# Attention and a gated MLP on one core: the first exponentials lie in another tile's memory, and the work is ordered anew

## The chip, the cores and the metric

The kernel runs on one core of a Trainium2 chip. Its engines work side by side, each through its own list of instructions in a fixed order: TensorE (PE; PEld is its weight load) multiplies matrices, VectorE (DVE), ScalarE (ACT) and GpSimd (POOL) work on tiles, and SyncE (SP) starts the DMAs. An instruction that must wait holds up all that stand behind it on its engine. The metric is the time of one execution on the device in microseconds (us), and less is better.

## The reference

The inputs are eight batches of eight heads, with 576 positions of 64 numbers. Queries and keys are first rotated by position ("rope"), then comes attention, and its output is the input of a gated MLP whose weights are the same for all batches:

```python
scores = matmul(rotate(q), rotate(k).T) / 8          # 576 x 576 per head
attn = exp(scores - max(scores)); attn /= sum(attn) + 1e-9
x = heads side by side of matmul(attn, v)            # 576 x 512 per batch
h = maximum(x @ w_in, 0)                             # 512 -> 1024, halves u and v
v_n = (v - mean(v)) / sqrt(var(v) + 1e-6)            # over the 512 features
v_s = w_spatial @ v_n + b_spatial                    # over the 576 positions
out = (u * v_s) @ w_out                              # 512 -> 512
```

## The kernel before

Two heads are worked on together: a *pair*. There are 32 pairs, numbered i = 0 to 31, four to a batch, and after the fourth pair of a batch comes the MLP of that batch, whose products stand between the score tiles of later pairs.

*Pairs 0 to 3* go the plain way. Their scores are fp32 matmuls (L817). VectorE takes the maximum of a score tile (L839), ScalarE the exponential (L842). The exponentials must lie turned for the product with v; TensorE turns blocks of them with matmuls against an identity matrix (function `turned` inside `values_plain`), ScalarE or VectorE copies the result out of PSUM into a slot called `eh`, and TensorE multiplies it with v (L726).

*Pairs from 4 on* go another way. A query or key is split into a high part, rounded by ScalarE (L420, `round_hi`), and a low part, the rest, by POOL (L423, `rest_lo`); the parts lie stacked in three tiles named `stk`, where the keys' parts (`lk`) are copied by DMAs. Scores are L797. VectorE turns the exponentials in blocks of 32 x 32 within their tile `et` (L844), and the product with v is L757: 288 small matmuls in two pieces, whose left operand is `vr`, a copy of v for this pair that four DMAs fill, one for each group of 32 partitions, 320 KB each.

POOL also does the rope (L545, then the sum L549 of its two parts), normalises the attention output (L880), and takes the low parts of all MLP operands: weights `wi`, `wo`, spatial weights `wsp` with their tail `wt`, and the normalised values `vn` (function `norm`). The MLP's spatial product is L955, of `vn` with `wsp`.

*Loads.* SP issues every DMA in one order (L417; the first ones at L599). `st` is the load of a pair's queries (st6_0 of pair 6) or keys (st6_1).

*What sets the order.* The program first lists 4344 operations, each with what it reads and writes, and then carries them out in the order of a table of numbers, `ORDER`; each engine gets its instructions in that order, and a letter behind a number says which engine does an operation that two could do. The buffers are handed out in the same walk: a `Buf` names a pool, `SLOTS` says how many slots the pool has, and the table `HOME` says which slot a new buffer takes. A buffer that takes a slot waits until the last reader of the slot's previous buffer is done.

*The place of the change.* `turns` is one buffer of pool "vrep", the pool of `vr` for pairs from 4 on, which has one slot. In it lie the `eh` slots and, behind them, the identity. `vn` is a tile of its own. The first instructions of the program fill it with constants: POOL fills a piece of `wsp` with zeros, on which TensorE runs matmuls (`wake`, L1032) before its first scores.

Of the kernel before, what the change touches and what calls it, by code (L numbers as in the profile page):

```python
# [8 lines left out]
F32 = mybir.dt.float32  # L9
# [6 lines left out]
P = 128  # L16
# [17 lines left out]
    "stk": 3, "small": 3, "nmx": 3, "rt": 1, "sc": 2, "pm": 4, "eh": 6,  # L34
# [66 lines left out]
4 65 5 2 7 6 12 0 3 1 8 9 10 11 13 15 138 14 16 139 142 70 71 72 74 73 76 79 77 36 75 80 140 81 402 18 78 84 82 85 86 87 83 88 144 91 89 90 100 143  # L101
101a 45 145v 218 59 312 17 96 92 93 130 141g 220 219 308 147 19 20 112 97a 113a 150 21 22 313 94 314 310 309 95a 98 99a 109 103 315 151 148 104a 102
23 149 24 131 105 27 107 110a 37 132 152 106a 108a 126 111 155 123 38 153 127a 121 393 156 214 215 216 217 39 154 40 133 157 41 42 124a 118 122a 28
116 25 114 119a 160 158 117a 29 120 125 128 30 161 159 31 32 162 115 129 60 33 165 170 221 174 171a 167 166 163 164 172 175v 134 135 34 168 420 146
173a 176 177v 169 223 224 206 179 181 311 226 180a 185 182v 183 178 207 208 188 136 137 227 225 228 62 421 427 186a 184v 187 189a 202 428 46 47 229
230 231 232 48 411 43 44 190 191 203v 49 50 194 433 195v 431 316 192 299 51 434 26 193a 233 234 199 435 200a 197 198v 235 236 237 196 201 238 204 54
55 246 209 205 290 241 242 239 240 63 210 247v 243 244 245 282 255 252 253a 257 256v 250 248 251a 436 249a 258v 259 317 283 284 432 291 292 222 211
422 254 61 35 318 264 319 320 321 260v 212 261 262a 293 294 265a 322 285 263 295 323 429 430 747 296 270 213 437 273 324 325 268 266 274v 326 493 269a
271v 327 297 440 267 300 275 301 438 328 272 276a 329 330 331 278 302 277 279v 52 340 303 304 819 305 344 439 753 754 341a 332 345a 333 298 748 755
335 825 337 338 306 280 334 342 343v 441 336 445 446 339 756 346 444 286 442 449 53 281 287 347v 450 353 376 377 447 355 354a 378 356a 451 412 348 413  # L110
457 358 826 359a 351 453 362 458 352a 64 459 363a 452 349 350a 288 461 372 414 307 443 454 455 763 415 759 357 373a 416 364 365a 417 462 448 465 466
369 379 289 367 384 757 380 370a 368a 758 764 456 460 385 366 463 464 423 467 360 468 371 361 426 374 375 820 386 469 470 471 381 382 383 477 760 394
# [210 lines left out]
def tile_attention_gated_mlp(  # L323
# [21 lines left out]
    def T(shape, dt, name):  # L345
        return sb.tile(shape, dt, tag=name, name=name, bufs=1)
# [72 lines left out]
    def round_hi(hi, src):  # L419
        nc.scalar.activation(hi, src, AF.Copy)  # L420
# [702 lines left out]
```

## Time and profile before

| | us |
|---|---|
| three runs | 812.27, 815.41, 815.51 (median 815.41) |
| profiled execution | 813.5 |
| its span, of which the page and the trace tell | 811.7 |
| PE busy | 797.3 (98%) |
| PEld busy | 720.4 (89%) |
| POOL busy | 609.4 (75%) |
| DVE busy | 583.6 (72%) |
| ACT busy | 537.9 (66%) |

The trace is one execution. A time is counted from the start of the span. An engine's idle time matters only where the engine that is nearly always busy, here PE, ends up waiting for it. SPq and POOLq are the issue of instructions by SP and POOL. "<-" behind an instruction names what its engine last waited for, with the line that wrote it.

### The profile page before, as it was taken

What the parts mean: (1) busy time and instruction counts of PE and PEld (TensorE: products, weight loads), DVE (VectorE), ACT (ScalarE), POOL (GpSimd) and SP (SyncE); (2) the same over time, 40 slices, a digit from 0 to 9 for tenths busy, and PEclk for the clock granted to TensorE, in tenths of its full rate; (3) what the DMA queues carried; (4) which work ended last, traced back from release to release, by engine and by line L of the source; (5) the groups of instructions that cost most, each with busy time, mean ns of one, the idle gap of its engine ahead of it and who ended that gap; (6) DMA issues with size and microseconds to landing.
All of it is one profiled execution on the core that took longest, in us unless ns stands there. A gap on an engine that the chain in (4) does not pass through costs nothing.

```text
span 811.7 us, 30045 instructions
## 1 busy us (share of the span) xinstructions
PE 797.3 (98%) x12568; PEld 720.4 (89%) x12568; DVE 583.6 (72%) x1230; ACT 537.9 (66%) x1353; POOL 609.4 (75%) x507
## 2 busy tenths in 40 slices
PE   7999899999999999999999999999999999999998
PEld 3666599998999989999899999999899998999898
DVE  6989897877876588676866778776787767774410
ACT  4988788665875678565775668656686657664442
POOL 7899799976869778798688877887879786644231
PEclk9999999999999999999999999999999999999999
DMA  9456665667765666757746776666566675452101
GB/s 347 181 192 202 154 162 140 173 178 197 169 162 132 170 178 157 196 147 193 201 119 163 177 205 169 161 167 158 166 178 146 168 205 166 109 138 69 44 2 59
DMA packets 53817, 129.86 MB, mean 160 GB/s; under 512 B 7857, under 2 KB 9905, under 8 KB 53682
## 3 DMA queue, kind: packets, MB, share of 16 engines
q1 hardware_dynamic: 53138, 127.35, 57.8%
q8 instruction: 99, 1.62, 0.9%
q10 hardware_dynamic: 544, 0.59, 0.3%
q14 instruction: 36, 0.29, 0.1%
HBM read 93.55 MB, written 9.58 MB: 127 GB/s over the span
## 4 chain that ended last, share of the span: by engine, by line
PE 87%; POOL 4%; DMA 3%; DVE 3%; ACT 1%; issue 1%; SPq 0%; POOLq 0%; DVEq 0%
PE psum L797 16%; PE psum L757 15%; PE psum L955 13%; PE psum L970 13%; PE psum L914 12%; PE psum L937 11%; PE psum L726 2%; PE psum L817 2%; PE psum L680 2%; DMA st<-in_qk_dram 2%; DMA vr<-in_v_dram 1%; DVE nmx L839 1%; POOL st L545 1%; POOL st L549 1%; ACT et L842 1%
## 5 line engine op out<-in xcount | busy, mean ns | idle before, releaser
L842 ACT ACTIVATE et<-psum,nmx 128x576 f32<-128x576 f32 x288 | 212.5, 739 | 98.8 <-DVE nmx L839 96.6
L839 DVE TENSOR_REDUCE nmx<-psum 128x1 f32<-128x576 f32 x288 | 212.6, 744 | 87.6 <-PE psum L797 71.8
L844 DVE STREAM_TRANSPOSE et<-et 128x576 f32<-128x576 f32 x252 | 188.1, 762 | 33.3 <-ACT et L842 31.9
L545 POOL TENSOR_TENSOR st<-st,tabs 128x1152 f32<-128x1152 f32 x56 | 149.6, 2673 | 25.8 <-DMA st<-in_qk_dram 25.1
L757 PE MATMUL psum<-et,vr 32*64 32x144 f32 x8064 | 142.1, 285 | 1.8 <-DMA vr<-in_v_dram 1.8
L757 PEld LDWEIGHTS psum<-et,vr 32*64 32x64 f32 x8064 | 126.5, 130 | 13.6 <-issue 8.5
L955 PE MATMUL psum<-wsp,vn 128*128 128x288 f32 x768 | 127.5, 297 | 0.6 <-POOL wsp L423 0.3
L937 PE MATMUL psum<-x,wi 128*128 128x288 f32 x768 | 125.4, 297 | 0.0
L914 PE MATMUL psum<-wi,x 128*128 128x512 f32 x448 | 119.5, 395 | 0.0
L970 PE MATMUL psum<-g,wo 128*128 128x288 f32 x768 | 117.5, 296 | 0.0
L937 PEld LDWEIGHTS psum<-x,wi 128*128 128x128 f32 x768 | 110.7, 188 | 5.3 <-issue 2.0
L955 PEld LDWEIGHTS psum<-wsp,vn 128*128 128x128 f32 x768 | 110.1, 188 | 2.7 <-issue 1.4
L970 PEld LDWEIGHTS psum<-g,wo 128*128 128x128 f32 x768 | 107.2, 188 | 2.6 <-issue 1.8
L797 PE MATMUL psum<-stk 128*128 128x288 f32 x448 | 99.2, 303 | 1.7 <-ACT et L842 1.2
L797 PE MATMUL psum<-stk,stk 128*128 128x288 f32 x448 | 95.6, 295 | 0.0
L914 PEld LDWEIGHTS psum<-wi,x 128*128 128x128 f32 x448 | 78.7, 188 | 12.2 <-issue 1.2
L423 POOL TENSOR_TENSOR stk<-st,stk 64x512 fp32r<-64x512 f32 x56 | 71.9, 1283 | 20.2 <-ACT stk L420 8.8
L797 PEld LDWEIGHTS psum<-stk 128*128 128x128 f32 x448 | 72.7, 188 | 12.0 <-ACT et L842 4.2
L549 POOL TENSOR_TENSOR st<-st 128x576 f32<-128x576 f32 x56 | 79.9, 1427 | 2.8
L423 POOL TENSOR_TENSOR g<-u,g 128x288 fp32r<-128x288 f32 x64 | 51.0, 809 | 32.5 <-ACT g L420 31.0
L797 PEld LDWEIGHTS psum<-stk,stk 128*128 128x128 f32 x448 | 71.7, 188 | 0.0
L423 POOL TENSOR_TENSOR x<-x,x 128x576 fp32r<-128x576 f32 x64 | 54.5, 874 | 22.4 <-ACT x L420 22.1
(130 smaller groups left out, 1065.2 us busy)
## 6 DMA issues: line engine op xcount, KB each, us to landing
vr<-in_v_dram SPq DMA_DIRECT2D x116, 320.0 KB
st<-in_qk_dram SPq DMA_DIRECT2D x62, 576.0 KB
stk<-lk SPq DMA_DIRECT2D x168, 144.0 KB
out_dram<-ob SPq DMA_DIRECT2D x31, 288.0 KB
ws<-in_w_spT_dram SPq DMA_DIRECT2D x2, 576.0 KB
tabs<-in_tab_dram ACTq DMA_DIRECT2D x2, 288.0 KB
st<-in_qk_dram SPq DMA_DIRECT2D x2, 288.0 KB
wi12raw<-in_w_in_dram SPq DMA_DIRECT2D x1, 512.0 KB
```

The source lines that it names most:

```text
L423: eng.tensor_tensor(out=lo, in0=src, in1=hi.bitcast(F32), op=ALU.subtract)
L545: f = lambda e: e.tensor_tensor(out=st[j][:, cols], in0=st[j][:, cols], in1=tabs[:, cols], op=ALU.mult)
L549: f = lambda e: e.tensor_tensor(out=st[j][:, :S], in0=st[j][:, :S], in1=st[j][:, S:2 * S], op=ALU.add)
L757: nc.tensor.matmul(bank(g)[64 * h:64 * h + 64, EACH // 9 * (1 - h):EACH // 9 * (1 - h) + EACH], lhsT=vr[rows, b % 4, b // 4, h, :], rhs=e[ ...
L797: nc.tensor.matmul(pt[:, c * 512:c * 512 + HALF], lhsT=lhsT, rhs=rhs[:, c * HALF:(c + 1) * HALF], start=(n == 0), stop=(n == len(parts) - 1))
L839: op(DVE, 680, key + K_MAX, lambda: nc.vector.tensor_reduce(out=nmx.tile, in_=tops(), op=ALU.max, axis=AX.XY, negate=True), r=[pt], w=[nmx ...
L842: op(ACT, 750, key + K_EXP, lambda: nc.scalar.activation(weights(), tops(turn), AF.Exp, bias=nmx.tile, scale=1.0, accum_out=sm[:, to:to + ...
L844: op(DVE, 705, key + K_TURN, lambda: nc.vector.transpose(out=blocks(et, at), in_=blocks(et, at)), w=[(et, at)])
L914: nc.tensor.matmul(pm.tile, lhsT=lhsT, rhs=win[1, d][:, j, :], start=(d == 0 and n == 0), stop=(d == 3 and n == len(todo) - 1))
L937: nc.tensor.matmul(pm[:, :HALF], lhsT=win[0, d][:, i, f * P:(f + 1) * P], rhs=x[d][:, at:at + HALF], start=(d == 0 and n == 0), stop=(d == ...
L955: nc.tensor.matmul(pm[:, :HALF], lhsT=lhsT, rhs=rhs, start=(t == 0 and n == 0), stop=(t == 4 and n == 1))
L970: nc.tensor.matmul(pm[:, :HALF], lhsT=wout[d,][:, i, m * P:(m + 1) * P], rhs=gs[d][:, at:at + HALF], start=(d == 0 and n == 0), stop=(d == ...
```

## The change

The buffer `turns` moves from pool "vrep" to a new pool "vn" of one slot, which it shares with `vn`; `vn` becomes a `Buf` that the first rounding of the first MLP opens, and every later user of it names it among what it reads. There are eight `eh` slots in place of six. The tables `ORDER` and `HOME` are written anew, all of them; a line of each is shown.

```diff
-    "stk": 3, "small": 3, "nmx": 3, "rt": 1, "sc": 2, "pm": 4, "eh": 6,
+    "stk": 3, "small": 3, "nmx": 3, "rt": 1, "sc": 2, "pm": 4, "eh": 8, "vn": 1,
...
-4 65 5 2 7 6 12 0 3 1 8 9 10 11 13 15 138 14 16 139 142 70 71 72 74 73 76 79 77 36 75 80 140 81 402 18 78 84 82 85 86 87 83 88 144 91 89 90 100 143
+0 65 5 3 7 1 12 4 6 10 8 9 11 13 15 14 16 2 70 71 72 73 74 75 138 140 139 76 79 80 77 78 81 86 84 85 384 91 82 83 87 88 100 89 90 142 143 144 101a 17
...
-    "00115400600472600176574110650011762253147160402567345176254564570654702645061"
+    "156400117230546070401657031657002145710316522407531642725644756041754036547610"
...
-    vn = T([P, 4, 2, HF], F32R, "vn")
+    vn = Buf("vn", [P, 4, 2, HF], F32R, "vn")
...
-                    need = [("vn", t, 0), ("vn", t, 1), ("wsp", t)] if t < 4 else [("vn", 4, 0), ("vn", 4, 1), ("vn", 4, 2), "wt", "ones"]
+                    need = [vn, ("vn", t, 0), ("vn", t, 1), ("wsp", t)] if t < 4 else [("vn", 4, 0), ("vn", 4, 1), ("vn", 4, 2), "wt", "ones"]
...
-            op(ACT, 520, key, lambda: round_hi(vn[:, t, 0, :], vv.tile), r=[vv], w=[("vn", t, 0)])
-            pair_op(HF, key, lambda e: rest_lo(e, vn[:, t, 1, :], vv.tile, vn[:, t, 0, :]), r=[vv, ("vn", t, 0)], w=[("vn", t, 1)])
+            op(ACT, 520, key, lambda: round_hi(vn[:, t, 0, :], vv.tile), r=[vv, *([vn] if b or t else [])], w=[("vn", t, 0), *([] if b or t else [vn])], new=[] if b or t else [vn])
+            pair_op(HF, key, lambda e: rest_lo(e, vn[:, t, 1, :], vv.tile, vn[:, t, 0, :]), r=[vv, vn, ("vn", t, 0)], w=[("vn", t, 1)])
...
-    turns = Buf("vrep", [P, 6 * CW + P], F32, "turns")
-    ident = lambda: turns[:, 6 * CW:]
+    turns = Buf("vn", [P, 8 * CW + P], F32, "turns")
+    ident = lambda: turns[:, 8 * CW:]
```

Where the instructions stand now is shown at two places. A number behind a name tells buffers of one name apart, and differs between the two programs.

**The four fetches of pair 4's vr, on SP.** In the order before they stand late and two at a time, between copies of pair 5's key parts (stk out of lk5); st6_1 is the load of pair 6's keys:

```order
L417 DMA rb3_931<-rt3d_826 64x576 x2
L417 DMA vr4_948<-in_v_dram 32x4x640 x2
L417 DMA st6_1_967<-in_qk_dram 128x1152
L417 DMA stk0_396<-lk5_893 64x576
L417 DMA stk2_398<-lk5_893 64x576
L417 DMA stk1_397<-lk5_893 64x576
L417 DMA vr4_948<-in_v_dram 32x4x640 x2
L417 DMA stk1_397<-lk5_893 64x576
L417 DMA stk0_396<-lk5_893 64x576
L417 DMA stk2_398<-lk5_893 64x576
L417 DMA st7_0_1280<-in_qk_dram 128x1152
```

In the new order two of them stand here, among early loads of weights (ws2, wi00raw) and of the values of pairs 2 and 3:

```order
L417 DMA ws2_280<-in_w_spT_dram 128x2x576
L417 DMA vr2_318<-in_v_dram 128x640
L417 DMA vr4_352<-in_v_dram 32x4x640
L417 DMA wi00raw_354<-in_w_in_dram 128x1024
L417 DMA rt0d_266<-rt0_267 2x4x128
L417 DMA rt0d_266<-rt0_267 2x1x64
L417 DMA vr3_374<-in_v_dram 128x640
L417 DMA vr4_352<-in_v_dram 32x4x640
```

and the fourth here, ahead of st6_1 again (the third stands between the two places, by itself):

```order
L417 DMA stk0_426<-lk5_925 64x576
L417 DMA wst_1013<-in_w_spT_dram 64x576 x2
L417 DMA wst_1013<-in_b_sp_dram 1x576
L417 DMA st7_0_1024<-in_qk_dram 128x1152
L417 DMA stk2_428<-lk5_925 64x576
L417 DMA stk1_427<-lk5_925 64x576
L417 DMA vr4_352<-in_v_dram 32x4x640
L417 DMA st6_1_1155<-in_qk_dram 128x1152
```

Three fetches have moved from behind pair 4's loads to far ahead of them, and the load of pair 7's queries, st7_0, now stands ahead of the last fetch and of pair 6's keys.

**POOL, the ropes after pair 5's query parts.** In the order before the rope of pair 6's keys (L545, st6_1) stands behind the low part of pair 5's queries for the first of its two stacks (stk0):

```order
L423 TENSOR_TENSOR stk0_396<-st5_0_672,stk0_396 64x512
L545 TENSOR_TENSOR st6_1_967<-st6_1_967,tabs_64 128x1152
L423 TENSOR_TENSOR wo0_1039<-sgwo0_991,wo0_1039 128x512
L423 TENSOR_TENSOR wi03_1042<-sgwi03_886,wi03_1042 128x512
L423 TENSOR_TENSOR stk1_397<-st5_0_672,stk1_397 64x512
```

In the new one the rope of pair 7's queries (st7_0) stands in that place:

```order
L423 TENSOR_TENSOR stk1_427<-st5_0_656,stk1_427 64x512
L423 TENSOR_TENSOR stk0_426<-st5_0_656,stk0_426 64x512
L423 TENSOR_TENSOR wo0_1022<-sgwo0_1005,wo0_1022 128x512
L545 TENSOR_TENSOR st7_0_1024<-st7_0_1024,tabs_64 128x1152
L423 TENSOR_TENSOR ql_74<-st6_0_760,qt_73 64x4x16 x2
L423 TENSOR_TENSOR wo1_1047<-sgwo1_1026,wo1_1047 128x512
```

The two ropes have changed places; that of pair 6's keys now follows four pieces behind it. At the start of the program the fill of the piece of wsp, which stood behind those of wt2, vt2, bias, sums, qt and ql, is now the first on POOL.

**POOL, ahead of the low part of pair 6's queries.** That part is the last row here (stk0<-st6_0). Before:

```order
L423 TENSOR_TENSOR wt2_70<-wst_865,wt1_69 64x576
L423 TENSOR_TENSOR vn_71<-vv0_0_1062,vn_71 128x512
L545 TENSOR_TENSOR st7_0_1280<-st7_0_1280,tabs_64 128x1152
L423 TENSOR_TENSOR wi02_1287<-sgwi02_1187,wi02_1287 128x512
L423 TENSOR_TENSOR lk6_1309<-st6_1_967,lk6_1309 128x576
L423 TENSOR_TENSOR ql_75<-st6_0_743,qt_74 64x4x16 x2
L549 TENSOR_TENSOR st7_0_1280<-st7_0_1280 128x576
L880 TENSOR_TENSOR x32_4_1271<-x32_4_1271,rb4_1334 128x576
L423 TENSOR_TENSOR stk0_396<-st6_0_743,stk0_396 64x512
```

Now:

```order
L423 TENSOR_TENSOR wsp_68<-ws0_820,wsp_68 128x576
L423 TENSOR_TENSOR vn_1176<-vv0_0_1063,vn_1176 128x512
L423 TENSOR_TENSOR wi02_1293<-sgwi02_1187,wi02_1293 128x512
L423 TENSOR_TENSOR lk6_1313<-st6_1_1155,lk6_1313 128x576
L423 TENSOR_TENSOR vn_1176<-vv0_1_1075,vn_1176 128x512
L549 TENSOR_TENSOR st7_0_1024<-st7_0_1024 128x576
L423 TENSOR_TENSOR wt2_70<-wst_1013,wt2_70 1x576
L423 TENSOR_TENSOR vn_1176<-vv0_2_1200,vn_1176 128x512
L880 TENSOR_TENSOR x32_4_1288<-x32_4_1288,rb4_1359 128x576
L423 TENSOR_TENSOR stk0_426<-st6_0_760,stk0_426 64x512
```

A piece of the spatial weights (wsp), two more pieces of the normalised values (vn) and the tail's one row (wt2, 1x576) have come ahead of it; the rope of pair 7's queries has left this stretch.

## Rows read from the trace of the kernel before

**Rows 1.** Stretches: us; PE, PEld, DVE, ACT, POOL busy; PEclk; DMA share; GB/s
```profile
0.00:20.00 20.00, 14.04 (x61) 7.23 (x62) 13.26 (x20) 9.83 (x21) 14.01 (x24) 1.00 0.91 346
20.00:40.00 20.00, 19.77 (x155) 12.01 (x152) 18.29 (x32) 18.23 (x48) 17.92 (x15) 1.00 0.49 180
...
80.00:100.00 20.00, 17.01 (x106) 11.76 (x104) 17.79 (x27) 14.65 (x36) 15.50 (x15) 1.00 0.65 164
100.00:120.00 20.00, 19.12 (x372) 17.25 (x373) 18.13 (x50) 16.67 (x42) 18.77 (x16) 1.00 0.61 151
120.00:140.00 20.00, 19.70 (x392) 18.38 (x391) 16.25 (x37) 16.70 (x45) 19.08 (x14) 1.00 0.49 135
140.00:160.00 20.00, 19.77 (x397) 18.80 (x396) 16.91 (x31) 12.52 (x30) 19.27 (x17) 1.00 0.66 169
160.00:780.00 620.00, 619.67 (x10572) 581.40 (x10571) 443.75 (x960) 406.87 (x1032) 461.78 (x378) 1.00 0.60 158
```

**Rows 2.** Waits of PE, 80 to 160 us: sum us, count, longest
```profile
PE psum L757 <- DMA vr<-in_v_dram: 1.8, 1, 1.8
PE psum L797 <- ACT et L842: 1.7, 2, 1.2
PE psum L955 <- POOL wsp L423: 0.3, 1, 0.3
```

**Rows 3.** Chain of waits around 93 us: start, duration, step
```profile
92.18 1.42 SPq L417
93.65 7.18 DMA vr<-in_v_dram
```

**Rows 4.** Timeline of SP: start, duration, instruction (x: how many in one row)
```profile
87.85 0.82 SPq L417 DMA_DIRECT2D vr<-in_v_dram  x2
88.78 0.96 SPq L417 DMA_DIRECT2D st<-in_qk_dram  x1
```

**Rows 5.** Timeline of PE; in brackets the idle time before, and its releaser
```profile
4.04 5.35 PE L1032 MATMUL psum<-wsp 128*128 128x512 f32 x8 [4.04 <-POOL wsp L388]
9.31 2.52 PE L817 MATMUL psum<-st,st 64*128 64x288 f32 x16
...
84.81 2.95 PE L726 MATMUL psum<-turns,vr 128*64 128x192 f32 x26
...
98.65 0.45 PE L757 MATMUL psum<-et,vr 32*64 32x144 f32 x2
100.88 2.90 PE L757 MATMUL psum<-et,vr 32*64 32x144 f32 x142 [1.77 <-DMA vr<-in_v_dram]
...
106.52 2.51 PE L757 MATMUL psum<-et,vr 32*64 32x144 f32 x144
...
123.77 0.43 PE L797 MATMUL psum<-stk 128*128 128x288 f32 x2
```

**Rows 6.** Chain of waits around 228 us
```profile
227.66 2.83 DMA vr<-in_v_dram
```

**Rows 7.** Timeline of VectorE
```profile
10.68 2.74 DVE L839 TENSOR_REDUCE nmx<-psum 128x1 f32<-128x576 f32 x4
...
97.59 0.76 DVE L844 STREAM_TRANSPOSE et<-et 128x576 f32<-128x576 f32 x1
```

**Rows 8.** Timeline of POOL
```profile
0.74 0.57 POOL L388 MEMSET wt<- 33x576 f32 x1 [0.29 <-POOLq L1111]
...
3.39 0.59 POOL L388 MEMSET wsp<- 128x576 f32 x1
...
96.65 2.67 POOL L545 TENSOR_TENSOR st<-st,tabs 128x1152 f32<-128x1152 f32 x1 [2.76 <-DMA st<-in_qk_dram]
...
107.20 1.28 POOL L423 TENSOR_TENSOR vn<-vv,vn 128x512 fp32r<-128x512 f32 x1
...
117.39 1.29 POOL L423 TENSOR_TENSOR stk<-st,stk 64x512 fp32r<-64x512 f32 x1
...
120.77 1.46 POOL L423 TENSOR_TENSOR wsp<-ws,wsp 128x576 fp32r<-128x576 f32 x1
```

More of the change, by code (lines that the diff above doesn't have):

```diff
@@ L100 @@
 ORDER = """
-4 65 5 2 7 6 12 0 3 1 8 9 10 11 13 15 138 14 16 139 142 70 71 72 74 73 76 79 77 36 75 80 140 81 402 18 78 84 82 85 86 87 83 88 144 91 89 90 100 143
-101a 45 145v 218 59 312 17 96 92 93 130 141g 220 219 308 147 19 20 112 97a 113a 150 21 22 313 94 314 310 309 95a 98 99a 109 103 315 151 148 104a 102
-23 149 24 131 105 27 107 110a 37 132 152 106a 108a 126 111 155 123 38 153 127a 121 393 156 214 215 216 217 39 154 40 133 157 41 42 124a 118 122a 28
-116 25 114 119a 160 158 117a 29 120 125 128 30 161 159 31 32 162 115 129 60 33 165 170 221 174 171a 167 166 163 164 172 175v 134 135 34 168 420 146
@@ L105 @@
[L105 to L112, printed above, removed]
[126 rows of a table removed]
+0 65 5 3 7 1 12 4 6 10 8 9 11 13 15 14 16 2 70 71 72 73 74 75 138 140 139 76 79 80 77 78 81 86 84 85 384 91 82 83 87 88 100 89 90 142 143 144 101a 17
@@ new lines @@
+145v 141g 96 97a 92 93 18 147 308 310 309 312 313 314 19 27 20 150 130 214 216 112 148 94 311 113a 95a 131 98 36 109 502 99a 110a 149 103 104a 21 22
+102 218 220 105 151 107 108a 106a 23 24 132 215 25 37 152 59 38 126 127a 155 156 153 39 154 40 62 121 41 122a 111 123 124a 42 28 157 315 222 160 60
+118 116 119a 117a 158 29 114 30 219 31 32 33 161 159 120 125 423 290 128 115 129 162 133 170 171a 316 165 166 163 164 424 174 299 146 167 175v 43 172
+134 45 176 168 169 173v 221 217 223 179 26 421 135 420 177v 136 137 185 224 180a 186v 226 225 183 206 184a 207 208 227 181 182v 34 188 178 46 47 189v
@@ new lines @@
+228 231 232 187 229 230 48 202 203a 190 427 428 435 436 44 194 195a 433 434 49 192 193a 233 191 50 51 197 198a 234 235 199 200v 236 431 196 201 432
+237 238 204 239 209 210 205 411 241 246 240 242 243 422 35 250 247v 63 244 245 248 282 249a 252 251v 257 255 253v 256a 317 258v 52 291 292 259 260a
+211 318 319 320 293 261 321 294 295 296 426 262a 254 264 322 323 747 748 402 265a 263 429 430 437 440 61 273 325 53 212 213 268 324 270 326 283 284
+285 269v 300 297 274v 266 438 327 271a 267 328 330 301 439 302 303 275 755 272 276a 278 277 329 304 279a 340 331 341a 344 345a 305 332 335 819 337 333
@@ L239 @@
+338 443 336 280 334 342 343v 445 346 339 376 446 441 286 449 347v 450 355 447 377 378 353 356a 54 451 348 354a 457 753 412 281 452 413 458 825 826 358
+359a 351 352a 442 393 448 298 459 453 454 379 754 414 415 349 416 362 363a 287 756 350a 461 364 455 456 417 757 758 372 365a 357 369 462 288 289 444
+465 466 373a 306 763 764 367 368a 366 370a 380 307 385 467 463 460 360 468 371 374 361 375 381 386 464 469 470 471 477 473 382 383 478 479 418 771 761
[126 rows of a table added]
 """
 HOME = (
-    "01070021200103201210302217010126030117512004364541564705001137041472110041753015520100670216130012427310017604554706201001264013005156201073"
@@ L242 @@
-    "54160267011010671524634550110740604100510301015071401201075063141152400120012271000721315440576050415011243305010143011752457400000416110115"
-    "04270103105401002011070400101100160210701512100061103004710100601002013071050411060070123701013146007210600170000114620005141017060051600402"
-    "10501017420101000000176010001151422073011015000014100011170003101650040310010112006511040100051001706010300141050046111013016214000500410020"
-    "05010001710650561047101000001572001000341107006410100501174003010010014020100000000711050401106030111000070140162007000001605010341100110070"
@@ L246 @@
-    "15016407020013005741421001000011067050611500014110001650040010200030511762001100341100700110041101070102100061010000017541100162031015300016"
-    "01000054110205040001760100102015042012703015404007300000116005114500110007161001540020020007041016005210021105010042060011051301000400011170"
-    "06104000001151102307130001400620070000160007015104010301061030117014020060000700115100004114701015060001470160060200070011000651410001210036"
-    "17110400100021107016000510001017101400010123000011654002105200400000013154761000111001161000007314062000000071150040411650011000060160452000"
@@ L250 @@
-    "11000001765102101407001004100630110400002107110060114003201150016130004110105236073001400076000001201054200170101062110004107101006100405117"
-    "00115400600472600176574110650011762253147160402567345176254564570654702645061"
+    "70001120010032012301202712006100111270161523464556042650107013630115460610405715127000170501662173602100700123060451560477650010107140720105"
+    "30741602031710600715246340115576011674701012007166501620130010570415042010021261106020315044365150407101147231746701017051432500010211176004"
@@ new lines @@
+    "42200370051410011200710004006100105111700113001012411001570004040000100116050074111000115110116402530420005030340000115020411007560100504100"
+    "01230056107041010001701160001105067003101021504000100001127000306115100410001200010165041000105300411070006110031500142401011605004000200500"
+    "04120072110601500115740000011576020003000041170601033100115400703010011400001020000071105000103406007111220001407300060010000715106014001000"
+    "10264701540120031520701004000011005671050011040101010645001026001003071641040111050021171010014001070000000021113600011705106011410002703015"
@@ new lines @@
+    "10000714000740000001265102107014000230010715424000700001163005014010516100701310005410110700400001106015201001410520611300041100210050001107"
+    "06120103051140100116210014030706000031006000710015041140601107011500002012400007000116200511700114510015240600070000010041100651170041011242"
+    "01500101600002150001340007100001165010100101023000652104100010450100011040157061001700111061021401370020200060100151040701410500601520041700"
+    "00000000116715001140061120530611001020510070010610015121001006410031050031040210076011400076000001500014000011006123701014000600070001145001"
```

252 rows, old and new, of the table ORDER are left out of this document.

## The prediction

> **What bounds the kernel now.** I read first the table of stretches [rows 1]. From 160 to 780 us TensorE is busy for 619.67 of 620 us: nothing can be won there, and a new order can only lose. Idle time that is not the start or the end lies between 80 and 160 us: 2.99 us in 80 to 100, 0.88, 0.30 and 0.23 us in the next three stretches, 4.4 us in all. In the same place POOL is nearly full too (18.77, 19.08 and 19.27 of 20 us from 100 to 160), so POOL is what could bind next.
>
> Then the waits of TensorE in that place [rows 2]: 1.8 us, once, for a DMA that fills vr; 1.7 us in two waits for an exponential (ACT L842); 0.3 us for POOL's low half of the spatial weights. The first is the place of this change. Tile vr is the copy of v for pair 4, the first pair that doesn't go by transposes. The chain of waits shows how it comes about [rows 3]: the DMA takes 7.18 us, from 93.65 to 100.83 us, and TensorE's products of pair 4 start right behind it.
>
> Why so late? In SP's timeline the first two of the four fetches of vr start at 87.85 us [rows 4]. The last matmul that reads turned exponentials (L726) runs from 84.81 for 2.95 us, to 87.76 us [rows 5]. The memory of vr is the one that holds the exponentials, so the first fetch can't be earlier. And SP issues in order: st, the load of pair 6's keys, stands behind it and goes at 88.78 us.
>
> **The change part by part.**
>
> *Where the exponentials lie.* They move into vn's memory, and vr's memory is free from the start. In the new order three fetches of vr stand far ahead, among loads of pairs 1 to 5, and only the fourth comes late, behind copies of pair 5's keys that wait for the last scores of pair 4. In before two such copies, of about half a microsecond each, stood ahead of the first late fetch, which SP issued at 92.18 us [rows 3]; now it is one. So the late fetch goes at about 91.6 us. Its landing is bounded by two rows: 2.83 us for a lone fetch of the same size at 227.66 us [rows 6], and 7.18 us [rows 3] plus its slow issue, 1.42 us, as it was in the crowd. That gives 94.9 to 100.2 us. I take a value nearer to the lone one, 96 to 98 us: of four fetches in the crowd (320 KB each) one is left, and pair 6's keys stand behind it now.
>
> What is late next? TensorE had done two matmuls of this product at 98.65 us, and stood [rows 5]. The other operand is the last of nine turned tiles, which VectorE gives at 97.59 + 0.76 = 98.35 us [rows 7]; between the maximum of pair 4's seventh score tile and that turn 13 VectorE instructions stand in both orders. So the product starts at 98.65 instead of 100.88: **-2.23 us**, and not more, even where TensorE comes earlier. If the fetch lands at its upper bound, 100.2 us, it is -0.7. The piece behind the wait took 2.90 us for 142 matmuls, and the next product, of 144, took 2.51 [rows 5]: **-0.4 us**, bounded by 0 and -0.4.
>
> *vn becomes a buffer that waits.* The first rounding into vn now waits for the last reader of the exponentials, at 87.76 us. In the trace of before POOL's first work on vn, which follows that rounding, is at 107.20 us [rows 8], some 18 us after the last reader. Cost 0; it would cost only if the MLP's first norm came 18 us earlier.
>
> *Eight slots for turned exponentials instead of six.* No wait of TensorE for such a slot is among its waits from 80 to 160 us; between 20 and 40 us it is busy for 19.77 of 20 [rows 1]. I take 0, bounds -0.2 and +0.2.
>
> *The order, start.* The fill that TensorE's warming matmuls wait for stood behind the other fills on POOL and is now first: it starts at 0.74 instead of 3.39 us [rows 8]. So these matmuls begin at about 1.4 instead of 4.04 us and end at 6.7 instead of 9.39 [rows 5]. The first scores can't use it: the first maximum runs on VectorE at 10.68 us [rows 7], behind VectorE's own rope of pair 0. So 0. But TensorE now stands idle between warming and first scores, for some 1.1 us. [...] Bounds 0 and +1.
>
> *The order, POOL.* Two changes work against each other. In before POOL stood for 2.76 us ahead of the rope of pair 6's keys, waiting for the load that SP held back [rows 8]. Now the rope of pair 7's queries stands there, with its load issued before the late fetch of vr: -2.76 us for POOL. On the other side four more pieces (a half of the spatial weights, two of vn, and the low part of the bias row) now stand ahead of the low part of pair 6's queries: 1.28 to 1.46 us each [rows 8], 5.4 us in all. It ended at 117.39 + 1.29 = 118.68; now 118.68 - 2.76 + 5.4 = 121.3. TensorE's first scores of pair 6 started at 123.77 [rows 5]; 2.6 us earlier is 121.1. Another 0.3 us I add for ACT copies that moved ahead of what POOL reads: **+0.5 us** of new wait. Bounds: 0, and +5 if POOL's idle time comes back (below). The wait of 0.3 us was for the second half of the spatial weights; that now follows one rope and one query part behind 121.3, so it ends near 127 us, some 6 us ahead of the first product that reads it: **-0.3 us**.
>
> *The rest of the order.* From 20 to 80 us the same matmuls stand in nearly the same order, and TensorE is near full; the two waits for exponentials (1.7 us) lie ahead of the product of pair 4, which waits for VectorE anyway. 0, bounds -0.7 and +1. After 160 us 0, bounds 0 and +1.5, since nothing idles there now.
>
> Sum: -2.23 - 0.4 + 0.5 - 0.3 = **-2.4 us**. The profiled execution took 813.5 us, its span 811.7 and 1.8 around it; it would take 811.1. The other three runs are 812.27, 815.41 and 815.51. The mean of all four is 814.2, and minus 2.4 that is 811.8 us, my time. It is a gain of 0.3%; what a measurement of this kernel can tell from no change is about 0.5%, or 4.1 us.
>
> **The rivals.**
>
> *All the idle time goes.* The eight slots and the new order take away the two waits for exponentials and the rest too, and VectorE's turns come as much earlier. For it: it is all one stretch, and VectorE's chain there begins with scores that wait. Against it: VectorE has 17.79 of 20 us there, and its order before the last turn keeps the same count. Price: 4.4 us of idle time [rows 1] and about 1 us in slow starts: 808.8 us from the mean.
>
> *The transfer stays late.* The change doesn't do what it says, since the fourth fetch still stands behind the copies that wait for pair 4's last scores, and it lands at 100.2 us or later. For it: that place in the order, and 7.18 us in the trace. Against it: three quarters of the bytes are gone from that time. Price: only -0.7, and +0.5 for POOL: 814 us.
>
> *POOL becomes the bound, slower than before.* The place is the low part of pair 6's queries. If POOL stands for its loads and for ACT as it did (2.76 us), the end is 118.68 + 5.4 = 124.1, and with 2 to 3 us of waiting for ACT's copies, of which five stand in new places, 126.5; TensorE wanted it at 121.1 and had it by 123.77. It decides from 123.8 us on. Each of pairs 7 and 8 then follows POOL, which has no idle time to catch up. Price: 2.7 us late, and as much again where the order later on has new waits in a stretch that had none: 817 to 819 us.
>
> **How the numbers follow.** The forecast has 0.52, all idle time gone 0.19, the late transfer 0.13, POOL 0.16. The forecast's own range is 809.5 to 814, by the bounds of the landing, the start and the runs' spread of 3 us. For 8 in 10 I leave out the best of the second case and the worst of the last: 807.2 to 816.8 us. Faster than 0.5% takes 810.1: nearly all of the second case and a tenth of the first, 0.23. Slower takes 818.3 or a POOL case with an unlucky run: 0.11. The rest, 0.66, is within 0.5%.
>
> **What would show it.** In the profile after: fetches of vr ahead of 60 us on SP; no wait of TensorE L757 for the DMA near 98 us; VectorE's last turn of pair 4 right before that product; POOL without the 2.76 us ahead of the first rope after 93 us; TensorE's idle time from 80 to 160 us at about 2 instead of 4.4 us. I'd be wrong if the L757 product still starts behind a DMA, if TensorE L797 waits for POOL's stk near 121 us for more than 1 us, if stretches after 160 us show idle time, or if the first maxima come later than 10.7 us.

## The result, and the profile after

The changed kernel took 825.28 us in the median of six runs (822.81 to 828.41), the kernel before 815.19 us in six runs beside it (812.27 to 819.34). The ratio is 1.0125, with a 95% interval of 1.0102 to 1.0148: slower by 1.25%, where 0.3% faster was forecast. The profiled execution has a span of 821.6 us, against 811.7.

The table of stretches answers to [rows 1]; the columns are the same:

```profile
0.00:20.00 20.00, 15.03 (x58) 7.96 (x60) 12.57 (x20) 9.99 (x21) 13.74 (x24) 0.91 0.90 337
...
80.00:100.00 20.00, 18.26 (x234) 13.67 (x237) 18.92 (x32) 18.30 (x46) 16.84 (x18) 1.00 0.60 163
100.00:120.00 20.00, 19.98 (x281) 17.79 (x265) 19.64 (x48) 17.58 (x43) 19.77 (x14) 1.00 0.58 154
120.00:140.00 20.00, 19.27 (x388) 17.70 (x387) 14.57 (x37) 14.08 (x36) 15.44 (x12) 1.00 0.47 135
140.00:160.00 20.00, 18.64 (x384) 17.30 (x383) 16.91 (x32) 11.61 (x29) 18.11 (x15) 1.00 0.46 116
160.00:780.00 620.00, 612.86 (x10502) 573.11 (x10502) 440.03 (x952) 402.29 (x1018) 458.88 (x376) 1.00 0.59 158
```

Read the last row first: TensorE idles for 7.1 us between 160 and 780 us, where it had idled for 0.33. From 80 to 120 us it idles less, 1.8 against 3.9 us, as the change meant it to, and from 120 to 160 more, 2.1 against 0.5. Together that is 3.9 us against 4.4, where the prediction looked for about 2. The granted clock of the first 20 us is 0.91. The waits of TensorE from 80 to 160 us answer to [rows 2] (sum, count, longest); the one for vr is gone, and the second and third are new:

```profile
PE psum L797 <- ACT et L842: 1.7, 2, 1.2
PE psum L955 <- DVE sgwo L467: 1.3, 1, 1.3
PE psum L797 <- POOL stk L423: 0.6, 1, 0.6
PE psum L797 <- issue: 0.2, 1, 0.2
```

From 380 to 780 us no wait of TensorE stood in this table before. Now there are these; a wait for `issue` is one for nothing that the trace shows:

```profile
PE psum L797 <- ACT et L842: 2.3, 2, 1.3
PE psum L955 <- POOL vt L423: 1.5, 1, 1.5
PE psum L955 <- ACT u L940: 1.2, 1, 1.2
PE psum L970 <- POOL g L423: 0.8, 1, 0.8
PE psum L757 <- issue: 0.3, 1, 0.3
PE psum L937 <- ACT vv L988: 0.2, 1, 0.2
```

To see when the time is lost, take in TensorE's timeline the start of the second piece of each pair's product with v (L757), and subtract the start of the same piece before. Negative is earlier, in us; each column is one execution:

| pair (its time before) | changed kernel | old order, new memory | new order up to pair 14, then old |
|---|---|---|---|
| 4 (106.5) | -3.3 | -2.9 | -3.9 |
| 5 (130.1) | -2.3 | -2.9 | -2.9 |
| 6 (155.6) | -0.4 | -3.2 | -2.8 |
| 8 (203.1) | -0.6 | -3.0 | -2.9 |
| 12 (298.2) | -0.6 | -3.7 | -2.3 |
| 16 (392.0) | -0.6 | -3.8 | -0.9 |
| 18 (441.8) | 2.5 | -3.8 | -1.0 |
| 22 (534.8) | 5.6 | -3.8 | -0.9 |
| 27 (650.4) | 7.0 | -3.8 | -0.3 |
| 31 (744.3) | 8.3 | -3.8 | 0.1 |

The last two columns are experiments, below. The changed kernel gains 2 to 3 us at pairs 4 and 5, gives most of it back by 155 us, holds 0.6 us up to 392, and then loses 8.9 us in steps. The waits listed above make some 6 of these 8.9 us; the rest stands in no row of waits. The end adds 1.6 to that (9.9 in the span).

### The profile page after: what moved, and what is told of

Same layout as the page of the kernel before. It is cut to its first block, busy times and chain, and to the rows that moved or that the text cites. A ratio compares the mean times of both kernels' runs of the same rounds, so it can differ in the third digit from the quotient of the medians.

```text
span 821.6 us, 30064 instructions
## 1 busy us (share of the span) xinstructions
PE 800.9 (97%) x12568; PEld 722.3 (88%) x12568; DVE 582.5 (71%) x1229; ACT 539.8 (66%) x1354; POOL 609.2 (74%) x507
## 4 chain that ended last, share of the span: by engine, by line
PE 81%; POOL 7%; DMA 4%; ACT 3%; issue 2%; DVE 1%; SPq 1%; POOLq 0%; ACTq 0%; DVEq 0%
PE psum L797 15%; PE psum L757 14%; PE psum L955 13%; PE psum L970 12%; PE psum L937 10%; PE psum L914 9%; PE psum L726 3%; PE psum L817 3%; PE psum L680 2%; DMA st<-in_qk_dram 2%; DMA out_dram<-ob 1%; POOL st L545 1%; ACT et L842 1%; POOL vn L423 1%; POOL st L549 1%
## 5 line engine op out<-in xcount | busy, mean ns | idle before, releaser
L545 POOL TENSOR_TENSOR st<-st,tabs 128x1152 f32<-128x1152 f32 x56 | 149.3, 2667 | 28.8 <-DMA st<-in_qk_dram 27.6
L757 PE MATMUL psum<-et,vr 32*64 32x144 f32 x8064 | 142.9, 285 | 0.8 <-issue 0.8
L757 PEld LDWEIGHTS psum<-et,vr 32*64 32x64 f32 x8064 | 126.8, 130 | 13.3 <-issue 9.4
L970 PE MATMUL psum<-g,wo 128*128 128x288 f32 x768 | 119.2, 296 | 0.9 <-POOL g L423 0.8
L423 POOL TENSOR_TENSOR stk<-st,stk 64x512 fp32r<-64x512 f32 x56 | 71.8, 1281 | 27.7 <-ACT stk L420 18.1
```

Source lines behind the costliest of these rows:

```text
L423: eng.tensor_tensor(out=lo, in0=src, in1=hi.bitcast(F32), op=ALU.subtract)
L545: f = lambda e: e.tensor_tensor(out=st[j][:, cols], in0=st[j][:, cols], in1=tabs[:, cols], op=ALU.mult)
L757: nc.tensor.matmul(bank(g)[64 * h:64 * h + 64, EACH // 9 * (1 - h):EACH // 9 * (1 - h) + EACH], lhsT=vr[rows, b % 4, b // 4, h, :], rhs=e[ ...
L970: nc.tensor.matmul(pm[:, :HALF], lhsT=wout[d,][:, i, m * P:(m + 1) * P], rhs=gs[d][:, at:at + HALF], start=(d == 0 and n == 0), stop=(d == ...
```

## The experiments

The two orders number the same 4344 operations, so that either can be used with the new memory, whole or in part. `ORDER` and `HOME` go together in all of them, so what is called the order here includes the slots that the buffers take. The runs stand in several groups, each beside the kernel before, whose median was 814.38 to 815.41 us; a difference between two groups is good to about 1 us.

**The new memory with the old order.** The code of the changed kernel, with the tables of before (one entry for vn added to `HOME`).

```diff
-0 65 5 3 7 1 12 4 6 10 8 9 11 13 15 14 16 2 70 71 72 73 74 75 138 140 139 76 79 80 77 78 81 86 84 85 384 91 82 83 87 88 100 89 90 142 143 144 101a 17
+4 65 5 2 7 6 12 0 3 1 8 9 10 11 13 15 138 14 16 139 142 70 71 72 74 73 76 79 77 36 75 80 140 81 402 18 78 84 82 85 86 87 83 88 144 91 89 90 100 143
...
```

> Only the memory is changed: the identity and the turned exponentials lie in vn's memory, eight slots are declared, and the table of the order is the one of before (vn's new entry is added to the table of slots). Theory A (the new order behind 390 us is what costs): no loss, 812 to 816 us beside 815.2, TensorE's idle time from 160 to 780 us below 1 us, and the 1.8 us wait of L757 for vr's DMA shorter or gone. Rival B (the memory itself costs: vn as a buffer that waits, or other addresses): 822 us or more, like the changed kernel. Rival C (the start, with its slow clock): like A here, 812 to 816.

Measured: 811.53 us (809.65 to 812.93), ratio to before 0.9959 (0.9943 to 0.9975). It is faster than both kernels, and the fastest tried. In TensorE's timeline the first piece of pair 4's product answers to [rows 5]; it stands whole and waits for nothing:

```profile
98.37 2.51 PE L757 MATMUL psum<-et,vr 32*64 32x144 f32 x144
```

And the last stretch is as full as before:

```profile
160.00:780.00 620.00, 619.75 (x10576) 581.89 (x10575) 441.44 (x956) 405.14 (x1027) 459.28 (x375) 1.00 0.59 156
```

So rival B falls: the memory costs nothing, it gains 0.4%. This order uses only six of the eight slots, so the gain needs no more of them.

**The two orders spliced, at the product of pair 15.** First the new order and then the old, and the other way round.

```diff
-2263 1656 1966 1970 1663 2264 1657 1664
+1968 1654 1664 1969 1970 1645 1928 1929
...
```

> The changed kernel with its new order up to the product of pair 15 (about 365 us) and the order of before from there on. Theory A (the new order behind 390 us costs): 813 to 816 us, level with before, and no stall of TensorE over 0.5 us behind 390 us. Rival B (the memory costs): 822 or more. Rival C (the first part of the new order costs, with its stretch at the clock's lower level): 822 or more.

> The changed kernel's memory with the order of before up to the product of pair 15 (about 365 us) and the new order from there on. Theory A (the new order behind 390 us costs): 822 to 826 us, with the stalls of TensorE at the same places as in the changed kernel (about 400, 429, 516, 525 and 649 us). Rival B (the memory costs): also 822 or more, so this run alone does not part it from A. Rival C (the first part costs): 813 to 816.

Measured: 819.72 us (ratio 1.0068, 1.0049 to 1.0088) with the new order first, 822.23 (1.0093, 1.0063 to 1.0124) with the new order last. The second is as theory A has it in its time; of the five stalls that A names its trace has three (2.79 us at 432, 1.48 at 529 and 1.13 at 653 us). The first is not, by 4 us, and its timeline says why: a stall at the seam, which neither order has alone.

```profile
379.90 0.54 PE L797 MATMUL psum<-stk 128*128 128x288 f32 x2 [4.15 <-ACT et L842]
```

It was run again with a seam at 347 us, where one buffer and not two has to take another slot:

> The second run again with a cleaner seam: the new order up to the product of pair 14 (347 us), then the order of before; one buffer at the seam lies in another slot than in either order, against two. In the second run a stall of 4.15 us at the seam hid what the first part costs. Theory A (the first part of the new order costs what its trace shows against the old order in the new memory, 3.2 us at 386 us, and the tail of before adds nothing): 813.5 to 816 us, and no stall over 0.5 us behind 250 us. Rival C (the first part is what makes the later stalls, through the state it leaves): 819 us or more.

Measured: 813.97 us (812.09 to 814.83), ratio 0.9989 (0.9970 to 1.0008), within the range of theory A. Its longest stalls behind 160 us are 1.07 us inside L757 at 202 and 0.82 us at the seam at 349, the second above what was expected. Against the old order in the new memory the first part of the new order so costs 2.4 us (813.97 - 811.53), and the part behind it 11.3 us more (825.28 - 813.97). The run with the old order first agrees on the second part: 822.23 - 811.53 is 10.7 us. The 2.4 us is an upper bound for the order of the first part, since in the trace 1.3 us are lost at pair 9, with the stop at 202 us, and 1.5 at pairs 15 and 16, with the seam. Rival C falls.

**The warming matmuls late again.** In the new order the fill for them goes back behind the other fills.

```diff
-0 65 5 3 7 1 12 4 6 10 8 9 11 13 15 14 16 2
+65 5 2 7 12 0 3 1 4 6 10 8 9 11 13 15 14 16
...
```

> The changed kernel with one thing undone: the fill that the warming matmuls wait for stands again behind the other fills on POOL, so that these matmuls run up to the first scores. By the clock's reading (the gap between 6.5 and 8.1 us lets the clock fall to its lower level from about 11 to 14 us) the granted clock is 1.00 in all of 0 to 20 us. Theory A: the time stays within 1 us of the changed kernel's 825.3, since the tail costs. Rival C (the slow start costs, and is carried to the end): 3 us or more faster, 822 or less.

Measured: 823.95 us (820.43 to 826.33), ratio 1.0107 (1.0066 to 1.0149), 1.3 us under the changed kernel: a little more than theory A allows, less than the 3 us of rival C, and no difference that four runs can tell. The granted clock is 1.00 from 0 to 20 us, as expected. But the runs with the new order first and the one with the mended tail keep the early fill, and their traces show 1.00 there too: the fall, to 0.91 over these 20 us, stands in one of four traces with the early fill. So the early fill alone doesn't make the clock fall here, and most of the loss is there without a fall at the start.

**The tail mended at seven places.** Six instructions are moved and the last output takes another slot, each against a stall of the changed kernel. The chain of waits shows the pattern at the first of them (start, duration, step):

```profile
389.79 1.30 POOL stk L423
391.09 0.02 issue
391.11 0.33 SPq L417
...
391.54 6.75 DMA out_dram<-ob
...
398.38 0.60 ACT vv L988
398.98 0.73 ACT et L842 x2
399.71 0.04 issue
399.75 0.80 PE psum L797 x4
```

Nothing here is slow or full. SP waits with a key's load for POOL's last use of the slot; behind it stands the store of an output that was ready long before; the store takes 6.75 us; the tile `vv` has the store's slot, so ScalarE waits with its first write; behind that stands an exponential, and TensorE's scores wait for the PSUM that it reads. At 525 us it is shorter. POOL waits for a load, and the vt piece that TensorE needs stands behind the rope:

```profile
521.00 2.68 POOL L545 TENSOR_TENSOR st<-st,tabs 128x1152 f32<-128x1152 f32 x1 [1.61 <-DMA st<-in_qk_dram]
523.76 1.26 POOL L423 TENSOR_TENSOR vt<-vv,vt 64x512 fp32r<-64x512 f32 x1
```

The edit, by pieces of the table (the store is 1711, the vt piece 2622 and the rope 3303):

```diff
-2464 2408 1711 2047 2315
+2397 2398 1711 2314 2355
...
-2955 2905 3303 2620 2664
+2918 2622 3303 2906 2920
...
```

> The changed kernel with seven instructions moved behind 380 us, one for each stall read there: on SP the store of an output goes ahead of the pair's small DMAs and of a key load that waits for POOL (stall of 1.0 us at 400 us); on POOL a sum goes ahead of the next pair's rope (1.3 us at 429), a vn piece ahead of a low part of x (1.2 us at 516), the vt piece ahead of a rope (1.5 us at 525), a piece of g ahead of a normalisation (0.8 us at 649); at the end one output is stored earlier and the last one takes another slot (1.3 us). Theory A (each stall is made by the place of one instruction): these stalls go and nothing takes their place, 817 to 820 us instead of 825.3. Rival D (POOL and ACT have no slack left in the new order, so a stall that is taken away comes back at the next pair): 822 us or more, with new stalls of TensorE within 30 us of the old places.

Measured: 818.37 us (815.64 to 822.12), ratio 1.0030 (1.0008 to 1.0053): 6.9 us less than the changed kernel, in the range of theory A. The first store now goes at 386.38, and ScalarE's write waits for no DMA:

```profile
386.38 0.35 SPq L417 DMA_DIRECT2D out_dram<-ob  x1
...
397.61 0.60 ACT L988 ACTIVATE vv<-psum 128x512 f32<-128x512 f32 x1 [0.30 <-PE psum L914]
```

The stalls at 400, 516 and 525 us are gone, and the wait for the store at the end. At 429 us 0.27 and 0.82 remain, and at 649 us one of 0.60 and a new one of 1.02 (for POOL's lk). So theory A holds for most of the tail by the runs, and rival D for two places of five. One trace doesn't account for the whole gain: it is of an execution of 820.78 us, in which TensorE also stops for 1.33 us inside L757 at 490 us, and it still loses 6.8 us between pairs 16 and 31, where the changed kernel loses 8.9.

**The first part mended too.**

```diff
-870 638 904 660 661
+653 654 904 503 504
...
-582 583 832 847 584
+804 798 832 561 607
...
```

> The run with the mended tail, and in the first part three more things: the warming matmuls late again; the low part of pair 6's queries ahead of two pieces that the new order put before it on POOL (stall of 0.56 us at 121.5 us); and a piece of g ahead of the second low part of pair 7's queries on POOL, which held up a weight's decoding on VectorE and by that TensorE (1.3 us at 152). Theory A: 2 to 3 us less than the run with the mended tail alone, 814 to 818 us, close to the order of before in the new memory (811.5). Rival D (no slack): no less than the run with the mended tail, stalls at other places between 120 and 200 us.

Measured: 816.49 us (813.76 to 817.27), ratio 1.0000 (0.9984 to 1.0016). It is 1.9 us less than with the tail alone, a little under what was expected. The stalls at 121 and 152 us are gone. What makes the rest, 5 us over the old order in the new memory (3 by the ratios), stays open.

**The old order with the early fetches.** New memory, old order, and three fetches of pair 4's vr (423, 424, 426) far ahead on SP. These are not the times of the new order: SP starts them in a bunch, at 54.4, 54.9 and 56.2 us, where the changed kernel has them at 18.1, 27.8 and 52.7, and the first run from 82 us on.

```diff
-463 464 423 467 360
+292 222 423 424 211
...
-371 361 426 374 375
+211 422 426 254 61
...
```

> New memory and old order as in the first run, and three of the four fetches of pair 4's vr at the early places that the new order gives them on SP. If the early places matter for the gain, L757 starts earlier than 98.4 us and the time falls below 811. If it was enough that the fetches no longer wait for the last reader of the exponentials: the same as the first run, 811.5 within 2 us, and L757 of pair 4 still starts at 98.4 us, since VectorE's last turn sets it. Rival: the early fetches crowd the first loads, and the first scores or the decoding of weights come later, 813 or more.

Measured: 815.52 us (811.59 to 822.46), ratio 0.9997 (0.9973 to 1.0022): 4 us more than without this move (3 by the ratios), and all of the gain is gone in the median. The time is that of the rival. The trace shows a place that the rival had not named, but it is of the slowest of the ten runs. On SP two of the fetches, with the v of pair 3 just ahead of them, stand before a key's load that the ropes want:

```profile
54.00 1.28 SPq L417 DMA_DIRECT2D vr<-in_v_dram  x3
55.84 0.35 SPq L417 DMA_DIRECT2D st<-in_qk_dram  x1
56.23 0.43 SPq L417 DMA_DIRECT2D vr<-in_v_dram  x1
```

The load takes 8 us:

```profile
55.84 8.02 DMA st<-in_qk_dram
```

POOL stands for its rope; in the first run it had no wait there:

```profile
63.92 2.63 POOL L545 TENSOR_TENSOR st<-st,tabs 128x1152 f32<-128x1152 f32 x1 [4.02 <-DMA st<-in_qk_dram]
```

At 69.5 us TensorE has stood for 3.2 us, and from 70 to 75 us the granted clock is 0.50, where the first run has 1.00:

```profile
69.52 2.05 PE L817 MATMUL psum<-st,st 64*128 64x288 f32 x5 [3.21 <-ACT et L842]
```

This trace is 8.5 us behind that of the first run at pair 4 and loses 4.2 more at pair 14 (see the end), while the medians are 4 us apart; how much of these 4 us is this wait is not shown. Two of the ten runs had a mean granted clock of 1.000, and took 811.59 and 814.07 us. The first run shows that it was enough to free the fetches. A bunch of them around another load cost 4 us here in the medians; the early places of the new order were not tried in the old one.

## Why the prediction was wrong

- *The fetch of vr* was right in its cause and a little small. L757 no longer waits for the DMA. By itself, with the old order, the term of -2.6 us measured -2.9 at pair 4, and 0.41% in the runs. In the trace a further 0.3 comes behind pair 5 with the wait for wsp, which is a term of its own, and 0.7 between pairs 9 and 10, whose cause is open. In the changed kernel it is -3.3 at pair 4, more than the prediction allowed: VectorE's last turns end at 97.90 us and not at 98.35, and the product starts at 97.77 without a wait:

```profile
97.77 2.76 PE L757 MATMUL psum<-et,vr 32*64 32x144 f32 x144
```

- *POOL and pair 6's low query* was right to a tenth, and by its mechanism: the wait of 2.76 us is gone, POOL works without a wait from 95.19 us to the end of that part, and the pieces that came ahead do the rest. +0.5 was forecast, with its end at 121.3 us. This row of the changed kernel's TensorE shows 0.56, and POOL's piece ends at 121.48. The wait of 0.3 us for wsp is gone, as forecast. The row:

```profile
121.53 0.53 PE L797 MATMUL psum<-stk 128*128 128x288 f32 x2 [0.56 <-POOL stk L423]
```

  The later losses are no lack of POOL's time either: it is busy for 458.88 of 620 us behind 160 us, less than the 461.78 of [rows 1].
- *The start* was right in its cost, 0. In the changed kernel TensorE stops at 6.5 us, and has three gaps before 10.92 us, of 1.65 us (some 1.1 was expected) and 0.47 in these rows and 0.83 behind them:

```profile
8.12 0.76 PE L817 MATMUL psum<-st,st 64*128 64x288 f32 x4 [1.65 <-DVE st L622]
9.34 0.76 PE L817 MATMUL psum<-st,st 64*128 64x288 f32 x4 [0.47 <-DVE st L631]
```

  The stretches of 2 us show a granted clock of 0.76 and then 0.50 behind them:

```profile
10.00:12.00 2.00, 1.17 (x8) 0.81 (x8) 1.97 (x4) 1.32 (x2) 1.39 (x8) 0.76 1.02 416
12.00:14.00 2.00, 2.00 (x10) 1.37 (x8) 1.25 (x3) 1.44 (x5) 2.00 (x2) 0.50 1.04 358
```

  The kernel before has no gap between the warming matmuls and the first scores [rows 5], and 1.00 in the first 20 us [rows 1]. The three other traces with the early fill have idle time at this place, 2.2 and 1.3 us between 6 and 12 us in the two runs with the new order first and 2.5 in the one with the mended tail, where the changed kernel has 2.9, and stay at 1.00, so that such gaps don't always bring the fall. The first transposes come at 18.39 instead of 17.53 us, and by 21.5 us 0.1 is left of it. No run shows the bound of +1 us as a loss that the start leaves: in its place the trace has 0.86 us at the first transposes and 0.1 at 21.5.
- *The rest of the order* is the step that failed. The prediction put it at 0, "bounds 0 and +1.5" behind 160 us, "since nothing idles there now". In the trace it measured 8.9 us from 392 to 744 us, 1.6 at the end, and 1.8 between pairs 5 and 6 (a piece of g behind two others on POOL held up VectorE's decoding, and TensorE for 1.3 us); by the runs the part of the order behind 347 us cost 11.3. The 1.8 is not fixed: in the two spliced runs that begin with the same order this step is 0.0 and 0.1. The bound of +1.5 was worked out from no row, though the prediction itself says that a new order can only lose there. A stretch with 0.33 us of idle time was taken as proof of slack; it is proof only that this one order fits. The new table has another order on SP, POOL and ScalarE in all of that stretch, and the prediction did not ask of it which instructions wait with others behind them.
- Of the rivals, the one that came out slower named POOL as the bound, in the same region as the first 1.8 us, with 817 to 819 us. Its "new waits in a stretch that had none" is what happened, at more than three times the price (8.9 us where it gave 2.7) and not by POOL being full.

## What to carry to other kernels

An engine that is busy for 99.9% of a long stretch is no cover for a new order: ahead of such a change go through each engine's new order for an instruction that waits on another engine or a load and now stands ahead of one that is needed at once. A change of memory and a new order should be timed apart, as here: the first was worth -0.41%, and the second took that back and three times more. A load that is freed from a wait need not be moved as well: here freeing brought the gain (811.53 us), and a bunch of three moved next to another load took it back (815.52).

## What was not expected of the hardware

In three traces a stall of TensorE cost one and a half times its length, or twice. Behind the 4.15 us at 379.90, in the first of the spliced runs, the granted clock fell to 0.50; the product of pair 15 is 2.0 us ahead of before and that of pair 16 4.2 behind, 6.2 us in all. In the same way 2.51 us cost 4.2 (below), and 1.68 us at 343 us in the run with the old order first cost 3.4, with a clock of 0.55 and 0.60 in the two stretches of 2 us from 344 us on. The first of the three:

```profile
380.00:382.00 2.00, 2.00 (x10) 1.81 (x11) 1.19 (x2) 1.27 (x4) 1.85 (x5) 0.70 0.07 25
382.00:384.00 2.00, 2.00 (x8) 1.81 (x7) 0.67 (x2) 0.43 (x2) 1.06 (x1) 0.50 0.00 0
```

Behind the stalls of 1.0 to 1.5 us from 390 us on, in the trace of the changed kernel, the granted clock stayed at 1.00. In the two other traces that have this tail unmended the stall near 430 us lasted 2.8 us instead of 1.3, the granted clock fell to 0.50 behind it, and 4.2 us were lost there; these two lose 11.1 and 11.2 us between pairs 16 and 31, against 8.9. And the pair of stalls near 90 us (1.19 and 0.5 us, in every run here) is followed by a granted clock of 0.50 in three of the ten traces, and of 1.00 in the others; whether this adds to the spread of the runs is not shown.

In eight of the ten traces TensorE stopped inside a product of L757, for 0.3 to 2.5 us, while it waited for nothing that the trace shows. The longest is in the run with the early fetches; a clock of 0.50 from 352 to 354 us followed, and the product of pair 14 lost 4.2 us:

```profile
351.54 1.24 PE L757 MATMUL psum<-et,vr 32*64 32x144 f32 x25 [2.51 <-issue]
```

The kernel before and the old order in the new memory show none. There are ten such stops, and in the list of TensorE's instructions, some 25300 in the trace, they stand at four places only: behind the first 5057 instructions (five traces), 9921 (two), 15041 (two) and 21697 (one). The distances between these are whole multiples of 256. A queue of the kind `instruction` has 99 packets of 16 KB each, which makes one for 256 of TensorE's instructions, if all of it is TensorE's (queue, kind: packets, MB, share):

```profile
q8 instruction: 99, 1.62, 0.9%
```

Each of the ten stops ended 1.3 to 1.6 us after such a packet had landed. So TensorE seems to have waited for its own next instructions; that is an estimate from these distances and times. L757 uses them up fast: 144 matmuls and as many weight loads in 2.51 us, where the other products in the trace of before come to some 68 matmuls in 10 us (3372 in the 493.6 busy us without L757, from 160 to 780 us). Why a packet comes late in one execution and not in another isn't shown; in the run with the early fetches the DMA share was full, 0.96 and 1.05, in the two stretches from 344 to 348 us, just ahead of the stop. No run here moves the packets.
